# Attention in a fused kernel: the second group's values loaded in the prologue, weights issued by ScalarE

## The chip, the cores and the metric

The kernel runs on one core of a Trainium2 chip. The metric is the device time of one execution in microseconds (us). Times inside an execution are counted from the start of its span, the stretch from its first to its last instruction. TensorE is the matmul engine, VectorE, ScalarE and GpSimd do elementwise work, and SyncE only issues DMAs and waits. In rows of the profile they are PE (PEld for its weight loads), DVE, ACT, POOL and SP; a q behind a name (SPq, ACTq) is the engine's queue of instructions, from which it issues DMAs.

## The reference

Windowed attention with global tokens, then two feed-forward networks without biases. Batch 4, 8 heads, 512 local and 32 global positions, head size 64; the networks have 2176 tokens, width 512 and hidden width 2048.

```python
k_all = concat([k_g, k_l]); v_all = concat([v_g, v_l])
out_g = softmax(scale * q_g @ k_all.T) @ v_all             # 32 global queries see all keys
s_ll  = where(abs(i - j) <= 32, scale * q_l @ k_l.T, -1e9) # local queries: a window of keys
s_lg  = scale * q_l @ k_g.T                                # and the global keys
out_l = softmax(concat([s_lg, s_ll])) @ concat([v_g, v_l])
x = concat([out_g, out_l]) as [2176, 512]
h = x @ w_in;  x = (h * cos(h)) @ w_out                    # first network
h = relu(x @ w2_in);  out = (h * h) @ w2_out               # second network
```

Inputs of the attention are fp32. The networks' weights come as 8-byte floats and are turned into fp32 on the chip from their two 4-byte halves.

## The kernel before, in words

The attention stage comes first, the networks after it. Attention works on groups of four heads: two groups per batch entry, eight in all (0 to 7). For each group the kernel loads keys (`load_k`, lines 252 to 259), queries (`load_q`, 261 to 265) and values (`load_v`, 267 to 276) from memory. `load_v` issues six DMAs into `VA`, the values in blocks of 128 rows that begin with the 32 global ones. `copy_v` (278 to 281) then makes `VB` from `VA` by two DMAs inside the on-chip memory: the same values in blocks shifted by half a block. A window of 128 keys that begins at a block's middle is then read as one block. `VA` and `VB` have two buffers each, so groups 0 and 1 use buffers 0 and 1, group 2 uses buffer 0 again, and so on.

TensorE works on pairs of heads: keys and queries are transposed through it (`tr_k`, line 295; `tr_q`, line 350), scores are made (line 400), the softmax runs on VectorE and ScalarE (lines 416 and 426), GpSimd and VectorE divide by the sums (line 456), the probabilities are transposed (line 469) and multiplied with the values of `VGZ` (line 485, global keys) and of `VA` and `VB` (line 497, windows). The work is cut into 40 items, five per group: two pairs of heads with two halves each, and one item for the group's global queries.

One loop (line 1362) writes the instructions of all engines in software-pipelined order. Step `s` makes the scores of item `s` and the softmax, the division of item `s - 1`, the transposes of item `s - 2`, the evacuations of item `s - 3` and the output of item `s - 4`. Each engine executes its own list in exactly this order. The order inside a step is `CFG['order']`. So the outputs of group 1, the first that read `VB[1]`, are in step 9, and the first that read the reloaded `VB[0]` of group 2 in step 14.

A prologue (lines 615 to 655) loads groups 0 and 1 before the loop, but of group 1 only keys and queries. Group 1's values are loaded at the end of step 2, and `copy_v(1)` follows at the end of step 5. Later groups are loaded by `LK`, `LQ`, `LV` and `CV` at fixed steps: the keys of group 2 in step 0 (`load_k(2)`), its queries in step 1 (`load_q(2)`), its values in step 8 and their copy in step 11.

Between the attention's work the loop carries the conversion of the first weights. `ATT` lists six pieces of 128 x 512 weights. `piece(i)` (line 1301) puts the load of piece `i` (`conv_load`, 512 KB, two buffers `raw0` and `raw1`) into step 5 + 3 * i or later, in slot `BG`, and its arithmetic into later steps: `conv_u` on GpSimd (line 142), `conv_s` on ScalarE (line 147), `conv_v` and `conv_o` on VectorE, `conv_c` on GpSimd. In slot `BG` of a step ScalarE stands behind the evacuations of that step (`TE`) and before its evacuation of keys (`KEV`) and its exponentials (`SM`). Weights that are loaded later go through `opQ` and a planner, which call the same `conv_load`.

All DMAs but a few of the prologue are issued by SyncE (`nc.sync`), in the order in which they are written.

Of the kernel before, what the change touches and what calls it, by code (L numbers as in the profile page):

```python
# [20 lines left out]
P = 128  # L21
# [31 lines left out]
def kernel(  # L53
# [14 lines left out]
    nc = tc.nc  # L68
# [38 lines left out]
    WI, WO = {}, {}  # L107
    nets = ((w1_in, w1_out), (w2_in, w2_out))

    def conv_load(q, m, c):  # L110
        g = 2 * q + c
        win, wout = nets[g // NC]
        f0 = (g % NC) * P
        t = convp.tile([P, DM, 2], I32, tag=f"raw{RJ[q, m, c][0]}", name="raw")
        flat = t.rearrange("p f w -> p (f w)")
        if m == 0:
            nc.sync.dma_start(
                flat.rearrange("p (k x) -> p k x", k=NK),
                win[:, 2 * f0 : 2 * f0 + 2 * P].rearrange("(k p) x -> p k x", p=P),
            )  # L120
        else:
            nc.sync.dma_start(flat, wout[f0 : f0 + P, :])
        raw[q, m, c] = t

    def conv_to(q, m, c):
# [8 lines left out]
    def conv_u(q, m, c, on):  # L134
        t = raw[q, m, c]
        u = conv_to(q, m, c)
        tmp[q, m, c, 0] = u.bitcast(U32)
        h = t[:, :, 1].bitcast(F32)
        if on == "A":
            A.activation(u, h, AF.Copy, scale=2.0**-112)  # L140
        else:
            G.tensor_scalar(u, h, 2.0**-112, 1.0, op0=ALU.mult, op1=ALU.mult)  # L142

    def conv_s(q, m, c):
        v = convp.tile([P, DM], U32, tag=f"cc{RJ[q, m, c][1]}", name="cc")
        tmp[q, m, c, 1] = v
        A.activation(v, raw[q, m, c][:, :, 0].bitcast(U32), AF.Copy, scale=2.0**-29)  # L147

    def conv_v(q, m, c):
        u = tmp[q, m, c, 0]  # L150
        V.tensor_scalar(u, u, 3, None, op0=ALU.logical_shift_left)  # L151

    def conv_o(q, m, c):
        t = raw.pop((q, m, c))
        v = tmp[q, m, c, 1]
        V.scalar_tensor_tensor(  # L156
            v, t[:, :, 1].bitcast(U32), 0x80000000, v,
            op0=ALU.bitwise_and, op1=ALU.bitwise_or,
        )

    def conv_c(q, m, c):
        u, v = (tmp.pop((q, m, c, i)) for i in range(2))
        G.tensor_tensor(u, u, v, op=ALU.add)  # L163
# [56 lines left out]
    BT, BG, BS, BO = (0, 1), (2,), (3, 4, 5), (6, 7)  # L220
# [20 lines left out]
    def whole(dst, src, c0, queues):  # L241

        n = dst.shape[2]
        if n == 2:
            for h, queue in enumerate(queues):
                queue.dma_start(dst[:, c0:4, h], src[h].rearrange("(c p) d -> p c d", p=P))
        else:
            for c in range(c0, 4):
                r = P * (c - c0)
                queues[0].dma_start(dst[:, c], src[:, r : r + P].rearrange("h p d -> p h d"))  # L250

    def load_k(gi, h=0, n=4, queues=(nc.sync, nc.sync)):
        b, g = gi // 2, slice(4 * (gi % 2) + h, 4 * (gi % 2) + h + n)
        if gi not in kn:
            kn[gi] = fp.tile([P, 4, 4, D], F32, tag="kn", name="kn", bufs=2)
        t = kn[gi][:, :, h : h + n]
        nc.sync.dma_start(t[0:SG, 0], k_g[b, g].rearrange("h p d -> p h d"))
        nc.sync.dma_start(t[SG:P, 0], k_l[b, g, 0 : P - SG].rearrange("h p d -> p h d"))
        whole(t, k_l[b, g, P - SG : SL - SG], 1, queues)

    def load_q(gi, h=0, n=4, queues=(nc.sync, nc.sync)):
        b, g = gi // 2, slice(4 * (gi % 2) + h, 4 * (gi % 2) + h + n)
        if gi not in qn:
            qn[gi] = fp.tile([P, 4, 4, D], F32, tag="qn", name="qn", bufs=2)
        whole(qn[gi][:, :, h : h + n], q_l[b, g], 0, queues)

    def load_v(gi):
        b, h0 = gi // 2, 4 * (gi % 2)
        va, g = VA[gi % 2], slice(h0, h0 + 4)
        nc.sync.dma_start(va[0:SG, 0], v_g[b, g].rearrange("h p d -> p h d"))  # L270
        for c in range(5):
            r0, r1 = (SG if c == 0 else 0), (SG if c == 4 else P)
            nc.sync.dma_start(
                va[r0:r1, c],
                v_l[b, g, P * c - SG + r0 : P * c - SG + r1].rearrange("h p d -> p h d"),
            )
# [357 lines left out]
    copy_v(0)  # L634
    load_k(1, 2, 2)
    load_q(1, 2, 2)
    nc.vector.memset(qgbd, 0.0)
    nc.gpsimd.memset(masks[0], 0.0)
    for h in range(2):
        s = slice(64 * h, 64 * h + 64)  # L640
# [505 lines left out]
    for s in range(NS):  # L1146
        K, b, q = steps[s]
# [136 lines left out]
    bg = {"BG": {}, "CB": {}, "CC": {}}  # L1284
    room = {e: dict.fromkeys(range(NI + 8), r) for e, r in (("V", 0.8), ("G", 1.3), ("A", 0.85))}

    def put(where, on, fn, first, *needs):
        s = max([first] + [x + 1 for x in needs])
        while True:
            fits = [(room[e][s] - d, e) for e, d in on.items() if room[e][s] >= d]  # L1290
            if fits:
                break
            s += 1
        e = max(fits)[1]
        room[e][s] -= on[e]
        bg[where].setdefault(s, []).append(lambda: fn(V if e == "V" else G))
        return s
# [3 lines left out]
    def piece(i, *needs):  # L1301
        k = ATT[i]
        s = max(5 + 3 * i, read.get(i - 2, 0) + 1)
        bg["BG"].setdefault(s, []).append(lambda: conv_load(*k))
        u = put("BG", {"G": 0.64}, lambda e: conv_u(*k, "G"), s + 3 + (i > 1), *needs)
        c = put("BG", {"A": 0.66}, lambda e: conv_s(*k), max(s + 3 + (i > 1), summed.get(i - 2, 0) + 1))
        v = put("CB", {"V": 0.41}, lambda e: conv_v(*k), u, c - 1)
        o = read[i] = put("CB", {"V": 0.68}, lambda e: conv_o(*k), u, c - 1, v - 1)
        summed[i] = put("CC", {"G": 1.28}, lambda e: conv_c(*k), s + 2, v, o)
        return summed[i]  # L1310
# [51 lines left out]
    for s in range(L["TRK"], NI + L["OE"]):  # L1362
        due = lambda k: due_tr.get(s - k)
        qe = []
        for c in CFG["order"]:
            if c in ("BG", "CB", "CC"):
                for fn in bg[c].get(s, []):
                    fn()
            elif c in ("TRK", "TRQ", "KEV", "KC", "QE"):
                p = due(L[c])  # L1370
                if p is None:
                    continue
                if c == "TRK":
                    if p == 0:
                        spin(6)
                    tr_k(p)
                    if p == 0:
                        spin(2)
                elif c == "TRQ":
                    qe = tr_q(p)  # L1380
                    if p == 0:
                        spin(2)
                elif c == "KEV":
                    k_evac(p)
                elif c == "KC":
                    k_copy(p)
                elif c == "QE":
                    for op in qe:
                        op()
            elif c in ("LK", "LQ", "LV", "CV"):  # L1390
                p = due(L[c])
                if p is not None and p % 2 == 0 and p // 2 + 2 < 2 * B:
                    dict(LK=load_k, LQ=load_q, LV=load_v, CV=copy_v)[c](p // 2 + 2)
            else:
                i = it(s - L[c])
                if not i:
                    continue
                if c == "S":
                    i.s_mm()
                    if s == 0:  # L1400
                        prep_ktail(0)
                        k_tail(0)
                        k_tail(1)
                    elif s % 10 == 6 and s < 30:
                        prep_ktail(s // 10 + 1)
                    elif s % 10 == 3:
                        prep_qg(s // 10)
                elif c == "SM":
                    for op in i.softmax():
                        op()  # L1410
                elif c == "RC":
                    for op in i.recip():
                        op()
                else:
                    dict(NM=i.norm, TM=i.t_mm, TE=i.t_evac, OM=i.o_mm, OE=i.o_evac)[c]()
        if s in (8, 18):
            load_ktn(s // 10 + 2)
        if s in (7, 17, 27):
            load_qgn(s // 10 + 1)
        if s == 2:  # L1420
            load_v(1)
        if s == 5:
            copy_v(1)
        if due(0) is not None and due(0) // NPAIR + 1 < B:
            if due(0) % NPAIR == 2:
                load_vg(due(0) // NPAIR + 1)
        if s == XBOPEN:
            first.close()
            open_pool("xb")
        if s == NI - 1:  # L1430
            early.close()
            open_pool("s")
        if s >= NI - 1:
            emit(1.55 * (s - NI + 2))
# [39 lines left out]
```

## Time and profile before

| | us |
|---|---|
| Median of 3 runs | 870.78 |
| Lowest and highest of the runs | 869.53 and 872.69 |
| Profiled execution, its own time | 871.06 |
| Its span, first to last instruction | 869.2 |
| TensorE busy in the span | 849.2 (98%) |
| VectorE, ScalarE, GpSimd busy | 646.5, 531.0, 583.7 |

The profile is of one execution; its own time is 0.28 us above the median of the runs, and its span 1.9 us below its own time. The busy shares are means over the attention stage, which ends near 140 us, and the networks, which fill the rest. The transfers under discussion all lie in the first 90 us.

### The profile page before, as it was taken

The numbers are of one execution on the slowest core, as the hardware profiler recorded it, in microseconds if no ns is written. First come the engines' busy times: TensorE is split into PE (matmuls) and PEld (weight loads), VectorE is DVE, ScalarE is ACT, GpSimd is POOL, SyncE is SP. The second block draws the span as 40 slices with busy tenths as digits, with TensorE's granted clock in tenths as the row PEclk, the third lists the DMA queues.
The fourth block names the chain that finished last, engine by engine and source line by source line (L and its number), as shares of the span: only waits on it lengthen the run. The fifth ranks groups of instructions, "written<-read, shape, count | busy, mean of one in ns | idle before, by whom it ended". The sixth has DMA issues, their size and how long they took to land.

```text
span 869.2 us, 17150 instructions
## 1 busy us (share of the span) xinstructions
PE 849.2 (98%) x6028; PEld 783.2 (90%) x6028; DVE 646.5 (74%) x1425; ACT 531.0 (61%) x1275; POOL 583.7 (67%) x666
## 2 busy tenths in 40 slices
PE   7899999999999999999999999999999999999998
PEld 5677778999999999999999998889898999898886
DVE  6589886999798777967688898896755777454544
ACT  5689787987776666666555867655544554443331
POOL 6579998899797554758367999975645647432221
PEclk9999999999999999999999999999999999999999
DMA  7899674547785578547727556566764677447733
GB/s 164 192 216 199 145 222 165 230 171 244 265 319 173 172 300 298 163 155 299 298 66 249 218 172 264 209 231 235 265 218 139 240 293 228 131 163 247 218 117 84
DMA packets 134261, 182.00 MB, mean 209 GB/s; under 512 B 60960, under 2 KB 114720, under 8 KB 134176
## 3 DMA queue, kind: packets, MB, share of 16 engines
q1 hardware_dynamic: 130736, 179.79, 62.8%
q10 hardware_dynamic: 3440, 1.11, 0.5%
q8 instruction: 48, 0.79, 0.4%
q14 instruction: 37, 0.30, 0.1%
HBM read 141.03 MB, written 35.65 MB: 203 GB/s over the span
## 4 chain that ended last, share of the span: by engine, by line
PE 86%; POOL 6%; ACT 3%; DVE 2%; issue 1%; SPq 1%; DMA 1%; POOLq 0%; ACTq 0%; DVEq 0%
PE y L940 40%; PE hb L848 16%; PE ha L848 10%; PE he L848 10%; PE s L400 2%; PE o L485 2%; PE o L497 1%; POOL g L172 1%; POOL wf L163 1%; POOL xs L172 1%; PE tw L469 1%; ACT pt L426 1%; PE tk L295 1%; PE tq L350 1%; POOL pt L456 1%
## 5 line engine op out<-in xcount | busy, mean ns | idle before, releaser
L172 POOL TENSOR_TENSOR g<-cr,g 128x384 fp32r<-128x384 f32 (+1 forms) x192 | 203.9, 1074 | 146.7 <-ACT g L899 141.2
L951 DVE TENSOR_TENSOR xt<-y,xt 128x384 f32<-128x384 f32 (+2 forms) x287 | 170.5, 596 | 96.4 <-PE y L940 94.6
L940 PE MATMUL y<-g,wo 128*128 128x384 f32 (+1 forms) x1152 | 219.1, 327 | 0.3 <-DVE wo L172 0.3
L940 PE MATMUL y<-wo,g 128*128 128x512 f32 x816 | 209.4, 393 | 0.0
L940 PEld LDWEIGHTS y<-g,wo 128*128 128x128 f32 x1152 | 194.0, 188 | 1.3 <-DVE wo L172 0.5
L940 PEld LDWEIGHTS y<-wo,g 128*128 128x128 f32 x816 | 150.0, 188 | 24.1
L848 PE MATMUL hb<-xs,wi 128*128 128x384 f32 (+1 forms) x864 | 166.4, 327 | 1.4 <-ACT cr L888 1.2
L848 PEld LDWEIGHTS hb<-xs,wi 128*128 128x128 f32 x864 | 146.8, 188 | 7.8 <-ACT cr L888 1.6
L848 PE MATMUL he<-xs,wi 128*128 128x384 f32 (+1 forms) x576 | 110.9, 327 | 1.6 <-DVE cr L891 0.8
L848 PE MATMUL ha<-xs,wi 128*128 128x384 f32 (+1 forms) x576 | 110.9, 327 | 0.8 <-DVE cr L891 0.7
L899 ACT ACTIVATE g<-cr 128x384 fp32r<-128x384 f32 (+1 forms) x192 | 93.9, 502 | 20.1 <-DVE cr L891 19.0
L163 POOL TENSOR_TENSOR wf<-wf,cc 128x512 uint32<-128x512 uint32 x64 | 88.3, 1386 | 25.6 <-DVE wf L151 18.2
L848 PEld LDWEIGHTS he<-xs,wi 128*128 128x128 f32 x576 | 98.0, 188 | 6.2 <-DVE cr L891 1.5
L848 PEld LDWEIGHTS ha<-xs,wi 128*128 128x128 f32 x576 | 97.6, 188 | 3.5 <-DVE cr L891 1.0
L885 ACT ACTIVATE cr<-cr,halfpi 128x384 f32<-128x384 f32 (+1 forms) x96 | 56.0, 594 | 11.8 <-DVE cr L880 10.5
L156 DVE SCALAR_TENSOR_TENSOR cc<-raw,cc 128x512 uint32<-128x512 uint32 x64 | 62.5, 983 | 0.0
L426 ACT ACTIVATE pt<-pt,st 128x160 f32<-128x160 f32 x128 | 53.3, 428 | 1.3 <-DVE st L416 1.3
L151 DVE TENSOR_SCALAR wf<-wf 128x512 uint32<-128x512 uint32 x64 | 49.8, 782 | 5.4 <-POOL wf L142 5.2
L147 ACT ACTIVATE cc<-raw 128x512 uint32<-128x512 uint32 x64 | 42.4, 669 | 18.5 <-DMA raw<-in_moe_w_in_dram 11.3
L856 ACT ACTIVATE s<-hb 128x384 f32<-128x384 f32 (+1 forms) x48 | 22.7, 473 | 48.7 <-PE hb L848 48.6
L416 DVE CUSTOM_DVE_ANT_0 pt<-s,mask 128x160 f32<-128x160 f32 x128 | 33.8, 320 | 14.9 <-PE s L400 12.5
L856 ACT ACTIVATE s<-he 128x384 f32<-128x384 f32 (+1 forms) x48 | 22.7, 472 | 32.3 <-PE he L848 32.2
(146 smaller groups left out, 1327.6 us busy)
## 6 DMA issues: line engine op xcount, KB each, us to landing
xs<-xs_T SPq DMA_DIRECT2D x48, 768.0 KB, 5.7
xs<-xs_B SPq DMA_DIRECT2D x36, 768.0 KB, 5.5
raw<-in_moe_w_in_dram SPq DMA_DIRECT2D x32, 512.0 KB, 5.4
raw<-in_moe_w_out_dram SPq DMA_DIRECT2D x32, 512.0 KB, 4.8
xs<-xs_T SPq DMA_DIRECT2D x24, 640.0 KB, 5.9
xs_T<-xs SPq DMA_DIRECT2D x16, 768.0 KB, 3.9
xs<-xs_B SPq DMA_DIRECT2D x18, 640.0 KB, 5.8
xs_B<-xs SPq DMA_DIRECT2D x12, 768.0 KB, 4.7
```

What stands on the lines that cost most here:

```text
L147: A.activation(v, raw[q, m, c][:, :, 0].bitcast(U32), AF.Copy, scale=2.0**-29)
L151: V.tensor_scalar(u, u, 3, None, op0=ALU.logical_shift_left)
L156: V.scalar_tensor_tensor(v, t[:, :, 1].bitcast(U32), 0x80000000, v, op0=ALU.bitwise_and, op1=ALU.bitwise_or,)
L163: G.tensor_tensor(u, u, v, op=ALU.add)
L172: eng.tensor_tensor(lo, x, hi.bitcast(F32), op=ALU.subtract)
L426: nc.scalar.activation(self.pt[:, u, :], self.pt[:, u, :], AF.Exp, bias=self.st[:, 0, u : u + 1], scale=-1.0, accum_out=self.st[:, 1, u : ...
L848: nc.tensor.matmul(out, lhsT=w[:, ws, c : c + P], rhs=xs[:, xh, kk, 0:n], start=start and k == 0, stop=k == 5, skip_group_check=True,)
L856: A.activation(self.sb[name], self.hold(bank_name), AF.Copy)
L885: A.activation(self.r[key], self.r[key], AF.Sin, bias=halfpi, scale=TWOPI)
L899: A.activation(GT[s, f][0][:, th * n : th * n + n], self.r[key], AF.Copy)
L940: nc.tensor.matmul(o, lhsT=l, rhs=r, start=k == 0, stop=k == 5)
L951: V.tensor_tensor(dst, y, dst, op=ALU.add)
```

## The change

`load_v(1)` moves from the end of step 2 into the prologue, behind the last loads of keys and queries there, and `copy_v(1)` moves from the end of step 5 to the end of step 3. `conv_load` gets an argument for the queue that issues it, and `piece` passes ScalarE's; the six loads of `ATT` keep their steps and their slot. Loads of weights that the planner places stay with SyncE.

```diff
-    def conv_load(q, m, c):
+    def conv_load(q, m, c, queue=nc.sync):
...
         if m == 0:
-            nc.sync.dma_start(
+            queue.dma_start(
                 flat.rearrange("p (k x) -> p k x", k=NK),
                 win[:, 2 * f0 : 2 * f0 + 2 * P].rearrange("(k p) x -> p k x", p=P),
             )
         else:
-            nc.sync.dma_start(flat, wout[f0 : f0 + P, :])
+            queue.dma_start(flat, wout[f0 : f0 + P, :])
...
     load_k(1, 2, 2)
     load_q(1, 2, 2)
+    load_v(1)
     nc.vector.memset(qgbd, 0.0)
...
         s = max(5 + 3 * i, read.get(i - 2, 0) + 1)
-        bg["BG"].setdefault(s, []).append(lambda: conv_load(*k))
+        bg["BG"].setdefault(s, []).append(lambda: conv_load(*k, queue=nc.scalar))
...
-        if s == 2:
-            load_v(1)
-        if s == 5:
+        if s == 3:
             copy_v(1)
```

## Rows read from the trace of the kernel before

**Rows 1.** The page: the chain that ended last, by engine

```profile
PE 86%; POOL 6%; ACT 3%; DVE 2%; issue 1%; SPq 1%; DMA 1%; POOLq 0%; ACTq 0%; DVEq 0%
```

**Rows 2.** Waits, 20 to 170 us: total us, times, longest us

```profile
PE o L497 <- DMA vb<-va: 3.1, 2, 2.8
...
ACT cc L147 <- DMA raw<-in_moe_w_in_dram: 1.6, 1, 1.6
```

**Rows 3.** Timeline of TensorE: start, us, instructions, [idle before]

```profile
30.20 0.66 PE L295 MATMUL tk<-ident,kn 128*128 128x128 f32 x4
...
39.16 0.48 PE L497 MATMUL o<-tws,vb 128*64 128x64 f32 x4 [2.82 <-DMA vb<-va]
...
42.53 0.97 PE L400 MATMUL s<-kT,qT 64*64 64x160 f32 x16
...
56.58 0.34 PE L497 MATMUL o<-tws,vb 128*64 128x64 f32 x4 [0.26 <-DMA vb<-va]
...
58.43 0.48 PE L400 MATMUL s<-kT,qT 64*64 64x160 f32 x2
59.15 0.77 PE L400 MATMUL s<-kT,qT 64*64 64x160 f32 x14 [0.24 <-ACT ptg L551]
```

**Rows 4.** Busy time by stretch: engines, then PEclk, DMA share, GB/s

```profile
38.00:39.00 1.00, 0.00 (x0) 0.00 (x0) 0.89 (x7) 0.30 (x2) 0.17 (x1) 1.00 0.41 86
...
41.00:42.00 1.00, 1.00 (x7) 1.00 (x6) 0.00 (x0) 0.42 (x1) 0.00 (x0) 0.50 1.10 246
...
43.00:44.00 1.00, 1.00 (x29) 0.78 (x22) 0.46 (x3) 1.00 (x4) 0.41 (x2) 1.00 0.86 264
```

**Rows 5.** Timeline of SyncE's issues: start, us for all of the row

```profile
20.13 0.45 SPq L257 DMA_DIRECT2D kn<-in_k_g_dram  x1
...
25.34 1.83 SPq L270 DMA_DIRECT2D va<-in_v_g_dram  x1
27.21 2.62 SPq L273 DMA_DIRECT2D va<-in_v_l_dram  x5
29.88 0.43 SPq L117 DMA_DIRECT2D raw<-in_moe_w_in_dram  x1
...
34.95 0.61 SPq L281 DMA_DIRECT2D vb<-va  x1
...
40.99 0.44 SPq L117 DMA_DIRECT2D raw<-in_moe_w_in_dram  x1
...
46.69 1.74 SPq L258 DMA_DIRECT2D kn<-in_k_l_dram  x1
...
50.65 0.60 SPq L281 DMA_DIRECT2D vb<-va  x1
```

**Rows 6.** Timeline of ScalarE: the first work of step 5

```profile
23.00 0.61 ACT L475 ACTIVATE tws<-tw 128x512 f32<-128x512 f32 x1
```

**Rows 7.** DMAs issued at 30.05, 35.05, 50.80, and all into kn: us to landing

```profile
raw<-in_moe_w_in_dram SPq DMA_DIRECT2D x1, 512.0 KB, 5.4
...
vb<-va SPq DMA_DIRECT2D x1, 256.0 KB, 4.1
...
vb<-va SPq DMA_DIRECT2D x1, 256.0 KB, 5.8
...
DMA to landing us min/median/max: 1.8/2.8/5.1
```

**Rows 8.** First 10 us: SyncE's waits, and two issues

```profile
SPq L379 <- DMA qn<-in_q_l_dram: 0.6, 1, 0.6
...
1.78 0.51 ACTq L246 DMA_DIRECT2D qn<-in_q_l_dram  x1
...
5.33 0.33 SPq L379 DMA_DIRECT2D qgn<-in_q_g_dram  x1
```

**Rows 9.** Busy time 59.2 to 82.9, and where the chain goes next

```profile
59.20:82.90 23.70, 23.66 (x390) 19.09 (x390) 20.70 (x92) 22.55 (x82) 21.20 (x38) 1.00 0.94 205
...
82.92 0.39 ACT kT L308
```

## The prediction, made before the changed kernel was run

> **What bounds the kernel now.** I read the page's chain first: 86% of the span runs through TensorE [rows 1]. A change to loads can therefore only pay where TensorE itself waits for one, and the view of waits over the attention stage is read for nothing but that. Among TensorE's waits one stands out: the output matmuls of line 497 wait for the copy of `VA` into `VB`, 3.1 us in two waits, 2.8 the longer [rows 2]. TensorE's timeline places them. The first ends at 39.16 after 2.82 us, at the first item that uses `VB[1]`; the second, 0.26 us, ends at 56.58, at the first item that uses the reloaded `VB[0]` [rows 3]. The stretches of one microsecond show what follows the first: the granted clock is 1.00 in the idle stretch, 0.50 (the lower of TensorE's two levels) at 41 to 42, and 1.00 again at 43 to 44 [rows 4]. The same list of matmuls, from the wait's end to the next scores, took 39.16 to 42.53, 3.37 us, there, and 56.58 to 58.43, 1.85 us, after the short wait [rows 3]. So the first wait costs 2.82 + 1.52 = 4.34 us.
>
> Why is that copy late? SyncE's timeline answers. Its issues follow each other almost without a gap (27.21 + 2.62 = 29.83, the next at 29.88), in program order, and 46 of them lie between 20.13 and 50.65, 0.66 us each [rows 5]. SyncE is behind the program: the first load of weights belongs to step 5, whose first work on ScalarE is at 23.00 [rows 6], and SyncE issues it at 29.88 [rows 5]. The second copy into `VB[1]` is issued at 34.95 and lands 4.1 us later [rows 5, 7]: 39.05, the end of the wait. The second copy of the next group is issued at 50.65 and lands 5.8 us later [rows 5, 7]: 56.45, the end of the short wait. Both waits have one cause, a queue that can't issue faster.
>
> **The change, part by part.** *Values of the second group, and their copy.* Nothing is added or removed, only order. Before, five loads of keys, four of queries and six of values fill 20.13 to 29.88 [rows 5]; after, the six come first. The last load of keys becomes the eleventh issue instead of the fifth, at about 27.21. Loads of keys land 2.8 us after issue in the median [rows 7], so at 30.0; their transposes start at 30.20 [rows 3] and take the last chunk last. That is covered by a few tenths; without cover it costs at most 5.1 - 2.8 = 2.3 us [rows 7]. The copies (now ahead of the keys of the third group) take the place of the load of weights: second issue at about 30.5, landing 4.1 later, 34.6. TensorE asks for it at 39.16 - 2.82 = 36.34. So this part does remove the wait, with 1.7 us to spare: -4.34 us at that place.
>
> *Six loads of weights on ScalarE's queue.* Each takes about 0.43 us from SyncE [rows 5]. Two of them stand ahead of the next group's copies; with a gap of 0.05 each, SyncE gets there 0.97 us sooner. On ScalarE six issues of 0.4 to 0.5 us are added (0.51 for its load at 1.78 [rows 8]). Four fall where ScalarE has idle time; it waited 1.6 us for the first weights alone [rows 2], and that wait goes. The last two fall where it is busy 22.55 of 23.70 us [rows 9], up to 0.9 us; TensorE is busy 23.66 of 23.70 there [rows 9], so I take zero and keep 0.9 for the range.
>
> *A wait that this adds.* The load at 5.33 into `qgn` waited 0.6 us for a landing in `qn`, a tile that it doesn't touch [rows 8]. Counted over both queues it is the fourteenth issue, and the `qn` load of 1.78 is the sixth. So the program hands its completion semaphores out in turn, eight of them, over both queues, and an issue waits until the load eight places before it has landed. A load of weights on ScalarE now takes such a place early. It lands 5.4 us after issue [rows 7]; eight of SyncE's issues last 8 x 0.66 = 5.3 us at its mean pace and 4.2 at 0.53 (2.62 for five, [rows 5]). SyncE would then stand 0.1 to 1.2 us behind each of the two loads, with all later loads queued behind it. I take 0.6 each, 1.2 in all; bounds 0 and 2.4. SyncE so gives back what it gained.
>
> *Where the stall goes.* Without the first wait TensorE reaches the second one at 56.58 - 0.26 - 4.34 = 51.98. The copies that it needs there are issued at 50.65 - 0.97 + 1.2 = 50.88 and land 5.8 later at 56.68; with the 0.13 us between landing (56.45) and start (56.58), TensorE goes on at 56.81, 0.23 us later than now. It has then stood idle for 4.8 us, longer than the 2.82 after which the clock fell, so I count the 1.52 us once more, now here. The short wait for ScalarE at 59.15 (0.24 us, [rows 3]) goes, since ScalarE has caught up. Sum: 0.23 + 1.52 - 0.24 = +1.5 us. From 59.2 to 82.9 TensorE has no slack [rows 9], so this arrives at 82.92, where the chain turns to ScalarE's evacuation of keys [rows 9]; I carry it whole to the end. On the profiled execution's 871.06 us that is 872.6; that execution was 0.28 above the median of the runs shown (870.78), so **872.3 us**.
>
> With no wait behind the weights and a landing after 4.1 us instead of 5.8, TensorE goes on at 49.68 + 4.1 + 0.13 = 53.91, and the sum is -2.67 + 1.52 - 0.24 = -1.4: 869.4. With 2.4 us of waits it goes on at 58.0, +2.7: 873.5. That is this case's own range. A measurement of this kernel can tell about 0.3%, 2.6 us, from no change; this case is no change.
>
> **Rivals.** *Slower.* The copies come later than that, through the weights. The fourth load of weights belongs to step 14, the same step as the wait for `VB[0]`, and on a queue of its own it no longer stands behind the copies (where it stands now) but runs with them. Its price is at most its landing less that of a small load, 5.4 - 2.8 = 2.6 us [rows 7]. With it the sum is 1.5 + 2.6 = +4.1 us, 874.9; it decides from 1.1 us of added lateness on, where the sum passes 2.6. The same end has a ScalarE that stands before a load of weights because the load eight places before it is still unissued on the late SyncE: its exponentials and evacuations of keys wait behind. For it speaks that SyncE is 6.9 us late (23.00 against 29.88); against it, that eight places are 5.3 us and that a late TensorE lets SyncE catch up.
>
> A rule of the Trainium skill bears on this rival (DMA: Bandwidth & Descriptors, Queues, rings and completion order): each DMA engine takes turns between the queues that have work for it, a packet at a time. By that rule the weights would share the engines with the copies, as this rival has it; in the trace ScalarE's queue is used at the start alone, so no row shows it at this place.
>
> *Faster.* The gain stays. The copies must land by 51.98, so be issued by 51.98 - 0.13 - 4.1 = 47.75, 2.9 us sooner than now, of which 0.97 is given. The other 1.9 could come from SyncE's long issues, 1.83 us at 25.34 and 1.74 at 46.69 against 0.43 [rows 5], 2.7 us above plain ones, if they came from crowding that the second queue relieves. Against it: they stand alone, with plain ones before and after. Whole, it gives 870.8 - 4.3 = 866.5 us.
>
> *The wait is not removed.* Keys or queries of the third group, now behind the values, stall TensorE at 30.2 by up to 2.3 us. TensorE is then less early at 56.58, still waits there, and the end is that of the likeliest case; it has no chance of its own.
>
> **How the numbers follow.** The stall moves on, no gain: 0.48. Slower: 0.27. Faster: 0.25. Nearly all of the first case lies within 0.3%, and a little of the third's partial gains too: faster 0.24, same 0.49, slower 0.27. The range takes in most of both rivals: 866.8 leaves out the full gain, about 1 in 10, and 875.5 the worst of the slower one, less than 1 in 10.
>
> **What would show it.** Right: no wait of line 497 near 36, the same wait of 3 to 6 us near 52 to 57 with a granted clock of 0.50 behind it, and the second copy into the reloaded `VB[0]` issued between 49.7 and 52. SyncE issues some load late, at the landing of weights that it doesn't use. Wrong: copies issued before 48 and no long wait of TensorE before 83 (faster), copies landing after 58, or ScalarE idle before its issue of a load of weights (slower).

## Result: 0.5% slower, by one longer stall

The changed kernel takes **875.6 us** in the median of six runs (874.80 to 878.61), the kernel before 871.19 in the six runs beside it: ratio 1.0051, 95% interval 1.0040 to 1.0062. The forecast was 872.3, range 866.8 to 875.5, no change the likeliest. The time lies just above the range, at what the rival "Slower" gave (874.9); its mechanism made only a part of it, as shown below.

| | before | after |
|---|---|---|
| Profiled execution, its own time | 871.06 | 875.33 |
| Its span | 869.2 | 873.5 |
| TensorE waits for `VB` near 36 to 39 | 2.82 | none |
| TensorE waits for `VB` near 52 to 60 | 0.26 | 7.43 |
| Clock granted behind that wait | 1.00 | 0.50 |

The chain still runs through TensorE alone, so what it lost must be a wait of its own. First the page's chain by engine (against [rows 1]), then the one row of its waits from 20 to 170 us that names `VB` (against [rows 2]; two waits, 3.1 us, before):

```profile
PE 86%; POOL 6%; DVE 3%; ACT 2%; issue 1%; DMA 1%; SPq 0%; POOLq 0%; DVEq 0%; ACTq 0%
```

```profile
PE o L497 <- DMA vb<-va: 7.4, 1, 7.4
```

TensorE's timeline of the changed kernel shows the places that [rows 3] shows of before:

```profile
30.07 0.66 PE L295 MATMUL tk<-ident,kn 128*128 128x128 f32 x4
...
36.04 0.29 PE L497 MATMUL o<-tws,vb 128*64 128x64 f32 x4
...
51.86 0.28 PE L497 MATMUL o<-tws,va 128*64 128x64 f32 x4
59.57 0.48 PE L497 MATMUL o<-tws,vb 128*64 128x64 f32 x4 [7.43 <-DMA vb<-va]
...
62.95 1.53 PE L400 MATMUL s<-kT,qT 64*64 64x160 f32 x16
...
65.58 0.66 PE L350 MATMUL tq<-ident,qn 128*128 128x128 f32 x4
```

At 30.07 the moved keys are there; at 36.04 there is no wait: the values part did what it was to do, and TensorE is some 4.2 us ahead. It asks for the reloaded `VB[0]` at 59.57 - 7.43 = 52.14 and gets it at 59.57, 2.99 us later than before (56.58). From there to the next scores takes 62.95 - 59.57 = 3.38 us, against 1.85 before [rows 3]: 1.53 more. The stretches of one microsecond say why. PEclk is the number behind the five engines; it falls while TensorE stands idle, and is at the lower level of the two while it catches up:

```profile
54.00:55.00 1.00, 0.00 (x0) 0.00 (x0) 0.00 (x0) 0.00 (x0) 0.64 (x2) 0.72 1.08 317
58.00:59.00 1.00, 0.00 (x0) 0.00 (x0) 0.00 (x0) 0.00 (x0) 0.00 (x0) 0.50 1.31 178
...
61.00:62.00 1.00, 1.00 (x6) 1.00 (x7) 0.37 (x1) 0.01 (x1) 0.00 (x0) 0.50 1.24 237
...
64.00:65.00 1.00, 1.00 (x20) 0.59 (x14) 0.47 (x3) 1.00 (x4) 0.00 (x0) 0.66 0.84 193
```

So at the next scores the lag is 2.99 + 1.53 = 4.52 us. The short wait for ScalarE behind them [rows 3] is gone, but nothing is gained by it, since these scores still run at the lower clock. The transposes of queries that follow stand here in the kernel before:

```profile
60.90 0.66 PE L350 MATMUL tq<-ident,qn 128*128 128x128 f32 x4
```

The lag there is 65.58 - 60.90 = 4.68 us, and the spans differ by 873.5 - 869.2 = 4.3. This one stall makes the loss; how some 0.4 us come back later is not traced. The question is why the copy into `VB[0]` came at 59.4.

SyncE's waits from 20 to 54 us, those for a DMA, and its timeline (against [rows 5]):

```profile
SPq L273 <- DMA raw<-in_moe_w_out_dram: 2.2, 1, 2.2
SPq L250 <- DMA raw<-in_moe_w_in_dram: 1.1, 1, 1.1
...
SPq L286 <- DMA raw<-in_moe_w_in_dram: 0.2, 1, 0.2
```

```profile
24.03 2.31 SPq L250 DMA_DIRECT2D kn<-in_k_l_dram  x3
27.52 2.02 SPq L250 DMA_DIRECT2D qn<-in_q_l_dram  x4
...
48.03 1.80 SPq L379 DMA_DIRECT2D ktn<-in_k_l_dram  x1
...
52.47 0.51 SPq L280 DMA_DIRECT2D vb<-va  x1
53.03 0.59 SPq L281 DMA_DIRECT2D vb<-va  x1
```

SyncE stands idle from 26.34 to 27.52, before a load of queries, for weights that this load doesn't touch; in all it stands 1.1 + 0.2 + 2.2 = 3.5 us behind three loads of weights. So the second copy goes out at 53.03 instead of 50.65 [rows 5]. The weights' issues on ScalarE are short; the first, third and fourth:

```profile
21.96 0.43 ACTq L117 DMA_DIRECT2D raw<-in_moe_w_in_dram  x1
...
41.63 0.35 ACTq L122 DMA_DIRECT2D raw<-in_moe_w_out_dram  x1
...
51.13 0.35 ACTq L122 DMA_DIRECT2D raw<-in_moe_w_out_dram  x1
```

Before, SyncE reached that third load only after the copies:

```profile
54.92 0.79 SPq L122 DMA_DIRECT2D raw<-in_moe_w_out_dram  x1
```

The landings, in the view of DMAs (KB, then us from issue to landing), of the fourth weights, of keys issued at 51.37, and of the two copies:

```profile
raw<-in_moe_w_out_dram ACTq DMA_DIRECT2D x1, 512.0 KB, 4.6
...
kn<-in_k_l_dram SPq DMA_DIRECT2D x1, 128.0 KB, 4.9
...
vb<-va SPq DMA_DIRECT2D x1, 256.0 KB, 5.9
...
vb<-va SPq DMA_DIRECT2D x1, 256.0 KB, 6.4
```

53.03 + 6.4 = 59.4, the end of the stall. The keys land 4.9 us after issue beside these weights, 2.8 in the median before [rows 7].

### The profile page after: what moved, and what is told of

It reads as the page before. It is cut to its first block, busy times and chain, and to the rows that moved or that the text cites. A ratio compares the mean times of both kernels' runs of the same rounds, so it can differ in the third digit from the quotient of the medians.

```text
span 873.5 us, 17136 instructions
## 1 busy us (share of the span) xinstructions
PE 851.7 (97%) x6028; PEld 785.4 (90%) x6028; DVE 645.0 (74%) x1425; ACT 530.4 (61%) x1275; POOL 583.2 (67%) x666
## 4 chain that ended last, share of the span: by engine, by line
PE 86%; POOL 6%; DVE 3%; ACT 2%; issue 1%; DMA 1%; SPq 0%; POOLq 0%; DVEq 0%; ACTq 0%
PE y L941 40%; PE hb L849 16%; PE ha L849 10%; PE he L849 10%; PE s L400 2%; PE o L485 2%; PE o L497 1%; POOL g L172 1%; POOL wf L163 1%; PE tw L469 1%; PE tk L295 1%; POOL xs L172 1%; DVE pt L416 1%; PE tq L350 1%; PE og L599 1%
```

## Experiments

My theory after the result: the weights on ScalarE's queue are the whole loss, by two ways, SyncE standing behind their landings and the fourth of them running beside the copies. The rivals: the moved values themselves cost it; or only one of the two ways matters. Each kernel was timed in five rounds against the kernel before on the same chip. "Next scores" is the start of the scores behind the second wait, the row at 58.43 of [rows 3]; profiles are of one execution, so a median can differ from them by some us, and they differ by up to 1.2 us before the first wait.

| kernel | next scores | median | before | ratio (95% interval) |
|---|---|---|---|---|
| changed kernel | 62.95 | 875.60 | 871.19 | 1.0051 (1.0040 to 1.0062) |
| values part alone | 56.43 | 870.16 | 871.09 | 0.9990 (0.9981 to 1.0000) |
| weights part alone | 62.68 | 876.11 | 871.09 | 1.0065 (1.0045 to 1.0085) |
| GpSimd's queue | 56.48 | 875.28 | 871.09 | 1.0050 (1.0031 to 1.0068) |
| first three on ScalarE | 61.13 | 874.12 | 871.22 | 1.0034 (1.0024 to 1.0044) |
| last three on ScalarE | 58.63 | 872.96 | 871.22 | 1.0025 (1.0010 to 1.0041) |
| values, weights early | 56.41 | 870.95 | 871.51 | 0.9995 (0.9981 to 1.0008) |
| first alone on ScalarE | 56.12 | 871.97 | 871.51 | 1.0015 (1.0000 to 1.0029) |
| copies first | 55.18 | 868.97 | 871.09 | 0.9976 (0.9963 to 0.9990) |
| copies first, ScalarE | 58.99 | 871.24 | 871.22 | 1.0007 (0.9991 to 1.0023) |
| copies first, weights early | 54.66 | 867.90 | 871.22 | 0.9963 (0.9952 to 0.9974) |

### Which part costs

**Values part alone.**

```diff
-lambda: conv_load(*k, queue=nc.scalar)
+lambda: conv_load(*k)
```

> The values part alone: the weights are issued by SyncE again. The theory (the loss over before comes from the weights on ScalarE's queue; the values part alone only moves the stall on): TensorE reaches line 497 at about 52.1; SyncE stands behind no weights, and the second copy is issued at about 50.6 as before, lands about 5.8 later at 56.4; a stall of about 4.4 us, half clock behind it once more, +1.3 us against before, ratio 1.0015, about 872.4. The rival (the values part itself costs, through the late loads of keys and queries or a copy pushed later by them): the stall is as long as in the changed kernel, 7.4 us, and the time 875.5, ratio 1.005.

Measured: 870.16, no slower than before; the rival is out. But the stall that I expected didn't come either. TensorE's timeline, then VectorE's, then the second copy on SyncE:

```profile
38.61 0.66 PE L295 MATMUL tk<-ident,kn 128*128 128x128 f32 x4 [1.05 <-DVE qT L356]
...
54.58 0.34 PE L497 MATMUL o<-tws,vb 128*64 128x64 f32 x4
```

```profile
37.21 0.62 DVE L151 TENSOR_SCALAR wf<-wf 128x512 uint32<-128x512 uint32 x1 [2.61 <-POOL wf L142]
...
37.88 0.67 DVE L356 COPY qT<-tq 128x512 f32<-128x512 f32 x1
```

```profile
48.92 0.60 SPq L281 DMA_DIRECT2D vb<-va  x1
```

The copy went out 1.7 us sooner than before (50.65), and TensorE came some 2 us later than I had put it. The wait of 1.05 us at 38.61 is a good part of that: VectorE stood 2.61 us for GpSimd's conversion of the first weights, the queries' copy stood behind that, and TensorE behind both. Another 0.66 us was there before 26 us (transposes of queries at 25.16, at 24.50 before). The copy landed 5.5 us after issue, at 54.4: at the 52.1 that I had expected TensorE would have waited for it. So there is one more load in SyncE's order with no slack, the first weights, and putting these on ScalarE did help at that place.

**Weights part alone.**

```diff
-    load_v(1)
...
+        if s == 2:
+            load_v(1)
-        if s == 3:
+        if s == 5:
             copy_v(1)
```

> The weights part alone: values of the second group are loaded in steps 2 and 5 as before. The theory (SyncE stands behind the landings of ScalarE's weights, and the fourth of them runs beside the copies): the wait of 2.8 us near 36 to 39 stays; the copies for the reloaded VB[0] land near 59.4 as in the changed kernel, against TensorE's arrival at about 56.3; so a second stall of about 3 us, with the clock lost a second time, 1.5: +4.3 us, about 875.5, ratio 1.005. The rival (the weights' queue does no harm, the order of the values does): no second long wait, about 870.5, ratio 0.9995.

Measured: 876.11, as the theory has it, at another place. Two waits of SyncE, the landing of the second copy into `VB[1]`, then TensorE's first long wait:

```profile
SPq L250 <- DMA raw<-in_moe_w_out_dram: 5.2, 1, 5.2
...
SPq L273 <- DMA raw<-in_moe_w_in_dram: 1.8, 1, 1.8
```

```profile
vb<-va SPq DMA_DIRECT2D x1, 256.0 KB, 6.1
```

```profile
42.60 0.48 PE L497 MATMUL o<-tws,vb 128*64 128x64 f32 x4 [5.05 <-DMA vb<-va]
```

Ahead of the copies into `VB[1]` SyncE stood 1.8 us behind the first weights. The second copy went out at 36.37, 1.4 us later than before [rows 5], and landed 6.1 us after issue instead of 4.1 [rows 7]: the second weights, issued by ScalarE at 32.68, were under way until 39.0. (The view of waits also names these weights for 2.3 us at line 280, but that issue, 33.99 to 36.32, had ended before they landed, so it was no wait for them.) The first wait grew from 2.82 to 5.05 us. The 5.2 us behind the third weights came after it; at the second place TensorE was so late that the copies were there but for 0.18 us. The weights' queue alone makes the loss.

### By which way

**GpSimd's queue.**

```diff
-conv_load(*k, queue=nc.scalar)
+conv_load(*k, queue=nc.gpsimd)
```

> The changed kernel with the six loads of weights on GpSimd's queue instead of ScalarE's. If SyncE's standing is a matter of completion semaphores shared between SyncE's and ScalarE's issues, and GpSimd's have others: no issue of SyncE ends its wait at a landing of weights, the second copy is issued at 49 to 50 instead of 53.03, the stall near 52 shrinks from 7.4 to between 3 and 5 us, time 871 to 873, ratio 1.000 to 1.002. If the loss is that weights and copies share the DMA engines (the rival): the copies are issued early but land late, more than 6 us after issue, stall 6 us or more, about 875, ratio 1.005. If GpSimd's issues are themselves long, its evacuations and sums come late, and TensorE shows waits for GpSimd.

Measured: no wait of SyncE for weights before 60; the second copy goes out at 50.33, 2.7 us sooner than in the changed kernel, and lands 4.2 us later. So SyncE's standing belongs to what its issues share with ScalarE's: in the packed traces the issues of these two use the same eight completion semaphores, in turn over both queues, and GpSimd's six loads use six others. The stall is 1.94 us, less than expected, and the next scores come at 56.48, 1.95 us ahead of before. The time is a miss, 875.28: the third condition of the expectation came true. TensorE's timeline at 54 and near 82, GpSimd's just ahead of it, and the clock behind:

```profile
54.63 0.34 PE L497 MATMUL o<-tws,vb 128*64 128x64 f32 x4 [1.94 <-DMA vb<-va]
...
82.10 0.30 PE L469 MATMUL tw<-ident,pt 128*128 128x128 f32 x1 [0.46 <-ACT cc L147]
83.03 1.02 PE L469 MATMUL tw<-ident,pt 128*128 128x128 f32 x3 [0.64 <-POOL pt L456]
```

```profile
79.67 0.83 POOL L117 DMA_DIRECT2D raw<-in_moe_w_in_dram  x1
80.53 1.29 POOL L163 TENSOR_TENSOR wf<-wf,cc 128x512 uint32<-128x512 uint32 x1
```

```profile
86.00:87.00 1.00, 1.00 (x20) 0.87 (x16) 0.96 (x6) 0.30 (x1) 1.00 (x3) 0.50 0.15 33
```

GpSimd's issue of 0.83 us stands ahead of work that TensorE waits for (0.64 us; the longest such wait before was 0.4), and two short waits are followed by half clock. That the issue makes the wait longer is read from this order, not tested. The span is 870.8, 1.6 us over before, so about 3.5 us went after 57 us. This profiled execution (872.57) is the shortest of its runs; what the median has above it no trace shows.

**First three loads on ScalarE.**

```diff
-conv_load(*k, queue=nc.scalar)
+conv_load(*k, queue=nc.scalar if i < 3 else nc.sync)
```

> The changed kernel, but ScalarE issues only the first three loads of weights, SyncE the last three. The theory (the loss is SyncE standing behind the landings of the three loads ahead of the copies: 1.1, 0.1 and 2.2 us in the changed kernel): SyncE stands there as before, 3.4 us in sum; the second copy for the reloaded VB[0] is issued at 52.5 to 53 and lands at 58 to 59; the stall near 52 is 6 to 7.4 us with the clock lost behind it; time about 875, ratio 1.004 to 1.005. The rival (the loss is the fourth load of weights, which runs beside the copies): with that load back behind the copies the stall is under 5 us, time about 872.5, ratio 1.002.

**Last three loads on ScalarE**: the same with the two queues exchanged.

> The other half: SyncE issues the first three loads of weights, ScalarE the last three, so the fourth load of weights still runs beside the copies. The theory (standing is the loss): SyncE stands behind no weights before the copies; they are issued at 48.5 to 49.5 as in the values part alone and land 5.5 later, 54 to 55, against TensorE's arrival near 54; stall under 1.5 us, time 870 to 871, ratio 0.999 to 1.000. The rival (sharing is the loss): the copies land 8 us after issue, stall over 3 us, time 873 to 875, ratio 1.003 to 1.005.

The first three separate the two ways. SyncE's longest wait, its second copy, the landings of keys issued at 51.50 and of that copy, and TensorE:

```profile
SPq L273 <- DMA raw<-in_moe_w_out_dram: 3.2, 1, 3.2
```

```profile
53.16 0.59 SPq L281 DMA_DIRECT2D vb<-va  x1
```

```profile
kn<-in_k_l_dram SPq DMA_DIRECT2D x1, 128.0 KB, 2.7
...
vb<-va SPq DMA_DIRECT2D x1, 256.0 KB, 4.5
```

```profile
57.75 0.48 PE L497 MATMUL o<-tws,vb 128*64 128x64 f32 x4 [5.25 <-DMA vb<-va]
```

The copy goes out at the same time as in the changed kernel (53.16 and 53.03), but lands 4.5 us later instead of 6.4, and the keys 2.7 instead of 4.9: without the fourth weights beside them they are 1.9 and 2.2 us faster. The stall falls from 7.43 to 5.25, between what theory and rival expected; the time is 874.12, by ratio two thirds of the changed kernel's loss. So both ways count, standing the larger part, sharing the smaller. How large the smaller is stays rough: the intervals of the two kernels overlap a little, and each landing is of one execution. In the other kernels the second copies at this place that landed before any weights were issued took 4.3 to 4.8 us (copies first, weights early).

The last three miss what they were for. In the profiled execution (875.18, above its median) TensorE is held 2.85 us near 38 by the late first weights (as in the values part alone) and so comes too late at the second place to tell anything; ScalarE is late with it and issues the fourth weights at 55.35, behind the copies (50.87) and not beside them. The loss, 872.96, is one group of keys further on: SyncE stands 5.6 us behind this fourth load, and TensorE waits for the copies that follow (rows of SyncE and of TensorE):

```profile
SPq L273 <- DMA raw<-in_moe_w_out_dram: 5.6, 1, 5.6
```

```profile
76.65 0.34 PE L497 MATMUL o<-tws,vb 128*64 128x64 f32 x4 [2.70 <-DMA vb<-va]
```

Before, that place had no wait. Standing costs there too.

### Where the stall goes when the weights do no harm

**Values, weights early**: the values part alone, and

```diff
-        bg["BG"].setdefault(s, []).append(lambda: conv_load(*k))
+        bg["BG"].setdefault(s if i else 1, []).append(lambda: conv_load(*k))
```

> The values part alone, all weights on SyncE, with the first load of weights moved ahead of the two copies (issue near 29.3 instead of 30.90, landing near 34.4 instead of 36.45), so that VectorE does not stand for it and TensorE loses nothing near 38. It tests the step that the prediction calls the stall moving on, which the values part alone could not, since TensorE came 2 us late by another wait. The theory: TensorE reaches the place of the second wait at about 52.3; the second copy is issued at about 48.5 to 50 and lands 4.5 to 5.8 later, 53 to 55.8; a stall of 1 to 3.5 us there, behind it the clock lost again where it is over 1 us; time 869 to 871.5, ratio 0.998 to 1.0005. The rival (the copies are there in time): no stall, time 867, ratio 0.9955.

**First alone on ScalarE**: the changed kernel with `queue=nc.sync if i else nc.scalar`.

> The changed kernel with only the first load of weights on ScalarE's queue and the other five on SyncE: the part of the weights' edit that helps, without the other two loads that SyncE stands behind. The theory: SyncE stands behind the first weights about 1.1 us near 26.3 and behind no others; no wait near 38; TensorE reaches the place of the second wait at about 52.2, the second copy is issued at 49 to 51 and lands at 53.5 to 56; a stall of 1.5 to 4 us with the clock lost behind it, time 870 to 872.5, ratio 0.999 to 1.0015, so well below the 874.1 of the first three loads there. The rival (one load in the other queue costs as much as three): 874, ratio 1.0035.

Both times lie in what the theory gave, 870.95 and 871.97; the mechanism wasn't quite it. In the profiled executions a part of the gain goes back, ahead of the copies. TensorE and ScalarE with the weights early, then TensorE with the first alone on ScalarE:

```profile
48.72 0.66 PE L469 MATMUL tw<-ident,pt 128*128 128x128 f32 x4 [1.25 <-ACT tws L588]
```

```profile
45.84 0.70 ACT L147 ACTIVATE cc<-raw 128x512 uint32<-128x512 uint32 x1 [2.07 <-DMA raw<-in_moe_w_in_dram]
```

```profile
48.44 0.66 PE L469 MATMUL tw<-ident,pt 128*128 128x128 f32 x4 [1.90 <-ACT tws L588]
```

Now the second weights, still behind SyncE's queue, hold ScalarE, and ScalarE holds TensorE. No copy of `VB` is waited for after that. So in these traces the stall moves on, to the load that comes next in SyncE's order. But the profiled executions, 868.66 and 868.41, are the fastest of their runs and still 2.4 and 2.7 us below that of before (871.06); the runs reach 875.01 and 876.39. What the medians have above the profiled executions, 2.3 and 3.6 us, no trace shows.

### A version that beats both

**Copies first**: the values part, the weights on SyncE, and the plan of loads with the copies of `VB` ahead of the keys that they stood behind.

```diff
-         'LQ': 1,
+         'LQ': 2,
...
-         'CV': 11},
+         'CV': 10},
...
-        if due(0) is not None and due(0) // NPAIR + 1 < B:
-            if due(0) % NPAIR == 2:
-                load_vg(due(0) // NPAIR + 1)
+        if due(4) is not None and due(4) // NPAIR + 1 < B:
+            if due(4) % NPAIR == 2:
+                load_vg(due(4) // NPAIR + 1)
```

> The values part with the weights on SyncE, and in the plan of loads the values of the next group and their copies moved ahead of the keys and queries of the same stretch (copies 10 steps ahead instead of 11 but before the keys, queries one more step ahead, values of the global half four steps later). The theory (the stall is only a place in SyncE's order, and the queue has room for it): the copies into VB[0] land at about 51 to 52, TensorE's arrival; the stall near 52 is under 1 us and the clock stays at 1.00, so the whole 4.3 us of the first wait are kept: about 866.5 to 868, ratio 0.995 to 0.997. The rival (SyncE is short of time as a whole, so that whatever is put behind is late instead): keys or queries of the third or fourth group stall TensorE between 52 and 70 by 3 us or more, time 870 to 873.

**Copies first, ScalarE**: the same with the six loads of weights on ScalarE's queue.

> The order with the copies first (868.97 with the weights on SyncE), and the weights on ScalarE's queue. The theory: SyncE stands behind three loads of weights for about 3.4 us less 1.0 for the loads that it need not issue; the copies are issued at about 50 instead of 47.84 and land at about 55; TensorE, without the wait of 1 us near 38 that the order with SyncE has, is there at about 52.1; a stall of about 3 us and the clock lost, time 870.5 to 872, ratio 0.9995 to 1.001. The rival (with the copies ahead of the keys there is room enough, and the early first weights only help): no stall near 52, time about 867, ratio 0.995.

**Copies first, weights early**: the weights on SyncE, and the edit of one line shown above.

> The order with the copies first, all weights on SyncE, and one edit more: the first load of weights is put ahead of the second group's queries, 4 us sooner (issue near 26.0 instead of 30.16). In the values part alone and with the copies first VectorE stands 2.6 us near 34.6 to 37.2 for GpSimd's first conversion of weights, the queries' copy stands behind that, and TensorE's keys wait 1.0 us near 38 with half clock behind, some 1.9 us in all. The theory: that wait goes and the clock stays up, -1.9 us against the copies first alone, about 867.0, ratio 0.995 to 0.996. The rival (TensorE then only reaches the next place sooner, or the weights slow the keys that land beside them): a wait for keys near 30, or a stall near 51 to 52 of 1.5 to 2 us, and the time stays at 869, ratio 0.9975.

Copies first gives 868.97, a little above its expectation, with an interval below 1: in the profiled execution (867.37, the fastest) nothing behind the copies came late, and TensorE's longest wait from 20 to 170 us is 1.0 us. With the weights on ScalarE the same order gives 871.24. That is the time of the theory, but not by its path, which had no wait near 38 and some 3 us near 52: in the profiled execution (874.32, 3.1 us above the median) TensorE waits 2.70 us near 38 and 1.08 at the second place. Both ways are seen apart. Sharing: the second weights are issued at 31.40, 0.16 us behind the copy into `VB[1]`, which lands 7.7 us after issue, against 4.8 in the changed kernel, and TensorE waits for it. Standing: SyncE is held 5.0 us by the third weights, and the second copy into `VB[0]` goes out at 53.20 instead of 47.84. The landing, TensorE's wait, and SyncE's:

```profile
vb<-va SPq DMA_DIRECT2D x1, 256.0 KB, 7.7
```

```profile
38.96 0.34 PE L497 MATMUL o<-tws,vb 128*64 128x64 f32 x4 [2.70 <-DMA vb<-va]
```

```profile
SPq L286 <- DMA raw<-in_moe_w_out_dram: 5.0, 1, 5.0
```

With the first weights early, TensorE has only short waits from 24 to 60, at the second place none:

```profile
52.86 0.29 PE L497 MATMUL o<-tws,vb 128*64 128x64 f32 x4
```

867.90 us, ratio 0.9963 (0.9952 to 0.9974): about 3.3 us of the 4.34 that the first wait cost. That is the best version here; from copies first alone (0.9976, 0.9963 to 0.9990) the intervals don't tell it apart, and the 1.9 us that I expected between them is not borne out. Half clock behind the wait near 38, which that expectation counts on, is not in the traces: with the copies first, and in the values part alone, the clock stays at 1.00 from 38 to 42, so the wait itself, 1.0 us, was all there was to win.

## Why the prediction was wrong

- **What bounds the kernel**: right. The loss is one wait of TensorE and the clock behind it, and nothing off TensorE's path.
- **Values and their copy**: right. Keys at 30.07 without a wait, the first copies early, no wait at 36.04 (expected 30.0 and -4.34 us).
- **ScalarE's issues cost nothing**: right, 0.35 to 0.45 us each, and none on TensorE's path.
- **A wait that this adds**: the step that failed, in its size. It said that SyncE "would then stand 0.1 to 1.2 us behind each of the two loads", 1.2 us in all, at most 2.4. It was 3.5 us, behind three loads: 1.1 + 0.2 = 1.3 behind the two that I had counted, near the 1.2, and 2.2 behind a third. I had counted the loads ahead of the copies in SyncE's order, where the third comes at 54.92; ScalarE runs on time and issues it at 41.63, so it too stands ahead of them. That moves the second copy from the forecast 50.88 to 53.03.
- **Where the stall goes**: right in kind and place, 52.14 against the 51.98 forecast, and the clock's price up to the next scores right, 1.53 against 1.52. The landing was the second term off: 6.4 us against the 5.8 taken, since the fourth weights ran beside the copies. The rival "Slower" priced that at up to 2.6 us, and the first three on ScalarE show 1.9 of it, against their landing of 4.5. Whether the 5.8 of before was already a crowded one stays open: weights go out 1.5 us before that landing (54.92 and 56.45), but with weights issued while they were under way four second copies took 5.2 to 5.8 us here, two others 3.8 and 4.2.
- **The sum**: +2.15 for the issue and +0.6 for the landing on the forecast of +1.5 make +4.3, the difference of the spans. That the sum meets it so closely is in part luck: the 0.24 us counted as gained were not (the lag is 4.68 behind the next scores), and about as much came back later. The kernel before, too, was 0.4 us slower here than in the runs that I had (871.19, 870.78): 872.3 + 2.75 + 0.4 = 875.5, and 875.6 was measured. The point that the rival "Slower" named, 1.1 us of added lateness, was passed by the standing alone (2.15); what it had named, the fourth weights beside the copies, made the smaller term (0.6).
- **The rival "Faster"**: wrong. SyncE's long issues did not go with the weights; one of 1.80 us stands at 48.03 in the changed kernel.
- **Where the stall goes, without the weights' harm**: the prediction had it at `VB[0]` in any case. Three kernels (values alone, weights early, first alone on ScalarE) show it at the first or the second weights, before `VB[0]` is asked for. Their intervals leave at most 0.2% of gain, so the step holds for the medians, and not in its detail; in the profiled executions 2.0 to 2.7 us of the 4.34 stay gained.

On the shared engines a page of the Trainium skill (DMA: Bandwidth & Descriptors, Issuing engines are not separate DMA queues) says that loads started by different engines run on the same DMA engines and interleave, and that issuing from several saves only the time to issue. The runs here agree on the sharing: beside weights a copy landed 1.9 us later. Of the issue they show more than a saving: 0.43 us a load [rows 5] left SyncE, and 3.5 us of standing came instead.

## What to carry to other kernels

Moving a load to another engine's queue doesn't only free the first queue: it also changes when the load is issued, what it runs beside, and, where both queues draw on the same completion semaphores, how long the first queue stands. Count the moved loads in the order of the engine that will issue them. And where a queue as a whole has little slack, removing one late load shows the next one; the cure was the order in the queue, with what is needed first ahead.

## What the hardware showed that I had not expected

- A wait of TensorE isn't followed by the lower clock by its length alone. In the first alone on ScalarE 1.90 us idle left the clock at 1.00 in every microsecond from 48 to 52, while two waits of 0.46 and 0.64 us in the kernel with GpSimd's queue were followed by 0.50. TensorE was even busier ahead of the fall (0.64, 0.30 and 0.93 of the microseconds from 81 to 84) than where none came (0.54, 0.00 and 0.56 from 46 to 49).
- A copy of 256 KB within the chip landed 7.7 us after issue when 512 KB of weights followed it 0.16 us later from another queue, and 4.8 when they followed 0.97 us later (issues at 30.37 and 31.34 in the changed kernel).

That doesn't take a second queue: with the values part and the weights early SyncE issued both, the weights 1.1 us ahead (29.43 and 30.55), and the copy landed 6.6 us after issue:

```profile
vb<-va SPq DMA_DIRECT2D x1, 256.0 KB, 6.6
```

In the twelve traces, from 15 to 90 us, six copies took over 6 us to land, and each had weights under way beside it.
